# A new front for an attention-and-feed-forward kernel: q and k in long packets, weights cast by the DMA, batch 1 loaded late

## The chip, the cores, the metric

The kernel runs on one core of one Trainium2 chip. Times are device microseconds (us) of one execution, the median of several; one profiled execution gives the trace. The kernel before took 403.1 us (two runs, 402.74 and 403.46). Its runs in the later sets of experiments lay between 400 and 408 us, so kernels are compared by ratios of runs made in the same rounds on the same chip.

## The reference, cut

```python
B, H, S, D = 8, 8, 576, 64
# attention, for each batch and head
out_d     = softmax(scale * mean4(q) @ mean4(k).T) @ mean4(v)         # tokens in fours, then repeated 4 times
out_local = softmax(where(|i - j| < 4, scale * q @ k.T, -1e9)) @ v    # a band of 7 tokens
x = (repeat4(out_d) + out_local) as 4608 tokens x 512                 # heads side by side
# feed forward
h = x @ w_in                      # 512 -> 2048
g = elu(h)
y = g @ w_out                     # 2048 -> 512
```

The feed-forward works on 9 blocks of 512 tokens; the attention makes 576 tokens per batch. So block 0 needs batch 0, block 1 needs batches 0 and 1, block 2 needs batches 1 and 2.

## The kernel before

The work of one pair of heads has fixed steps: load q, k, v (SyncE's queue), cast to fp16 (GpSimd), turn q and k on TensorE and copy them out (ScalarE, VectorE), scores on TensorE, exponentials on ScalarE, a mask on VectorE. Four pairs make a batch: then the denominators (TensorE), their reciprocal (VectorE), its spread over the partitions by a trip through memory, the outputs (TensorE, VectorE), and the sum `xt` on GpSimd, which is the input of the feed-forward. The order in which each engine is given its instructions is written down by hand as a list of times:

```python
def load(b, j):                                # seven DMAs per pair, packets of 256 bytes
    nc.sync.dma_start(out=q32[:], in_=rows(q, 0, NB, 0, QB))
    for src, dst in ((k, k32), (v, v32)):
        nc.sync.dma_start(out=dst[0:96], in_=rows(src, 0, NB, 0, QB))
        ...                                    # 3 tokens of halo on either side, two more DMAs each

def load_weights(i):                           # 16 pieces of 512 KB
    w32 = sb.tile([128, 1024], FP32, tag="w32", bufs=3, name="w32")
    ...
    nc.sync.dma_start(out=w3, in_=src)
    return lambda: nc.gpsimd.tensor_copy(out=to, in_=w3)

def mm1(t, fc):
    tag = "misc" if t < 2 and fc % 2 else "hp"     # four banks in blocks 0 and 1, two later
    hp = ps.tile([128, TBLK], FP32, tag=tag, bufs=2, name="hp")
    ...                                        # 4 matmuls, exp on ScalarE -> e, two VectorE steps -> gt
def mm2(t, i):
    ...                                        # 4 matmuls; every fourth: ScalarE copies op -> os
    nc.sync.dma_start(out=out[r : r + 128, :], in_=os_[:])

at(-100, first)                                # loads of pairs 0 to 2
for n in range(4): ...                         # casts of batch 0
for i in range(8): at(-95, wload, i); at(-95, wcast, i)
for j in range(3): at(-90, load, 1, j); at(-90, wload, 8 + j)
...
for b in range(B):
    base = start_of(b) - 26.5                  # b >= 1: the pairs of batch b run beside the blocks before
    slots, d0, o0 = SLOTS, 16.1, (22.5, 24.1)
    ...
```

The softmax here doesn't subtract the row's maximum and nothing guards it: scores larger than these inputs give would overflow.

## Time and profile before

| stretch of the kernel before | us | length |
|---|---|---|
| attention of batch 0, until the first matmul of block 0's `mm1` | 0 - 44.9 | 44.9 |
| `mm1` of block 0, with pairs of batch 1 | 44.9 - 71.7 | 26.8 |
| `mm2` of block 0, the rest of batch 1, half of batch 2 | 71.7 - 108.1 | 36.4 |
| block 1, until batch 2's denominators are done | 108.1 - 119.0 | 10.9 |
| block 1, until block 2's first matmul | 119.0 - 142.0 | 23.0 |
| blocks 2 to 8 | 142.0 - 401.8 | 259.8 |

The stretches are cut at instructions read from the trace. The first view is from the page of the kernel before: the span in 40 slices of 10.0 us, busy tenths of TensorE, its granted clock, the busy tenths of the DMA engines and the rate in GB/s.

```profile
PE   1465688687986899999999999999899899999996
...
PEclk9999999968999799999999999999999999999999
DMA  6998999965966980796199639926820310100112
GB/s 121 189 253 258 190 215 234 265 126 134 198 139 130 189 176 16 172 231 125 28 195 217 118 78 194 226 64 121 172 79 33 102 53 28 49 29 28 52 54 78
```

TensorE is full from the fifteenth slice on and has holes before; the DMA engines are busy through the whole front. The next view is the same cut into the six stretches: start and end, length, then busy us (and instructions) of TensorE, its weight loads, VectorE, ScalarE, GpSimd, then the granted clock, the mean share of busy DMA engines (the times of all packets are summed, so it can pass 1) and the rate in GB/s.

```profile
0.00:44.90 44.90, 20.86 (x249) 15.71 (x250) 11.92 (x21) 15.36 (x29) 20.64 (x28) 1.00 0.92 203
44.90:71.70 26.80, 22.32 (x152) 10.89 (x151) 22.13 (x37) 14.73 (x28) 16.14 (x21) 1.00 1.12 222
71.70:108.10 36.40, 29.23 (x301) 15.87 (x301) 16.84 (x28) 15.02 (x30) 17.78 (x23) 0.86 0.83 176
108.10:119.00 10.90, 9.84 (x130) 5.98 (x129) 8.28 (x18) 9.61 (x20) 6.92 (x9) 1.00 0.89 169
119.00:142.00 23.00, 17.53 (x176) 9.57 (x173) 17.57 (x33) 11.36 (x22) 8.22 (x12) 0.85 0.81 152
142.00:397.80 255.80, 253.22 (x2055) 127.60 (x2053) 177.69 (x327) 137.14 (x251) 69.03 (x94) 1.00 0.47 105
```

From 142 us on TensorE works 253 of 256 us: only the first 142 us can give much. The chain of waits in the front shows what they are spent on (start, length, what; cut to its longest pieces).

```profile
13.33 4.52 DMA q_105<-in_q_dram
...
23.91 4.83 DMA w_152<-in_moe_w_in_dram
...
28.80 1.07 POOL WI L119
29.89 5.04 DMA w_161<-in_moe_w_in_dram
...
36.05 6.50 DMA w_170<-in_moe_w_in_dram
...
42.61 1.00 POOL WI L119
...
43.69 2.34 POOL xt L352 x3
```

The first feed-forward input `xt` (line 352) is made at 43.69 us, right behind GpSimd's last weight cast (line 119), which waited for the last weight load.

### The profile page before, as it was taken

The numbers are of one execution on the slowest core, as the hardware profiler recorded it, in microseconds if no ns is written. First come the engines' busy times: TensorE is split into PE (matmuls) and PEld (weight loads), VectorE is DVE, ScalarE is ACT, GpSimd is POOL, SyncE is SP. The second block draws the span as 40 slices with busy tenths as digits, with TensorE's granted clock in tenths as the row PEclk, the third lists the DMA queues.
The fourth block names the chain that finished last, engine by engine and source line by source line (L and its number), as shares of the span: only waits on it lengthen the run. The fifth ranks groups of instructions, "written<-read, shape, count | busy, mean of one in ns | idle before, by whom it ended". The sixth has DMA issues, their size and how long they took to land.

```text
span 401.8 us, 8092 instructions
## 1 busy us (share of the span) xinstructions
PE 353.0 (88%) x3052; PEld 185.6 (46%) x3052; DVE 254.4 (63%) x460; ACT 203.8 (51%) x377; POOL 138.7 (35%) x184
## 2 busy tenths in 40 slices
PE   1465688687986899999999999999899899999996
PEld 1352345343553455555545554555454444444442
DVE  0134599732586797697778769886886585555510
ACT  1462157535385376747564855667375334444321
POOL 3365755460850581075028304820450050000000
PEclk9999999968999799999999999999999999999999
DMA  6998999965966980796199639926820310100112
GB/s 121 189 253 258 190 215 234 265 126 134 198 139 130 189 176 16 172 231 125 28 195 217 118 78 194 226 64 121 172 79 33 102 53 28 49 29 28 52 54 78
DMA packets 138082, 53.81 MB, mean 134 GB/s; under 512 B 122580, under 2 KB 131388, under 8 KB 138044
## 3 DMA queue, kind: packets, MB, share of 16 engines
q1 hardware_dynamic: 129420, 47.62, 55.0%
q10 hardware_dynamic: 8624, 5.68, 6.6%
q8 instruction: 24, 0.39, 0.4%
q14 instruction: 14, 0.11, 0.1%
HBM read 43.33 MB, written 9.95 MB: 133 GB/s over the span
## 4 chain that ended last, share of the span: by engine, by line
PE 67%; DMA 12%; POOL 6%; issue 4%; DVE 4%; SPq 3%; ACTq 2%; ACT 1%; POOLq 0%; DVEq 0%
PE op L388 29%; PE hp L368 25%; PE sc L204 2%; PE tk L186 2%; PE tq L176 2%; DVE e L374 2%; PE tq L171 2%; PE lg L325 2%; POOL xt L352 2%; DMA w_170<-in_moe_w_in_dram 2%; DMA rcb<-rd 2%; SPq L149 2%; ACTq L276 2%; DMA w_161<-in_moe_w_in_dram 1%; DMA w_207<-in_moe_w_out_dram 1%
## 5 line engine op out<-in xcount | busy, mean ns | idle before, releaser
L368 PE MATMUL hp<-xt,WI 128*128 128x512 f16 x576 | 150.9, 389 | 4.5 <-DVE gt L377 2.5
L388 PE MATMUL op<-WO,gt 128*128 128x512 f16 x576 | 147.7, 385 | 4.7 <-POOL WO L119 3.8
L373 ACT ACTIVATE e<-hp 128x512 f16<-128x512 f32 x144 | 85.7, 601 | 109.5 <-PE hp L368 90.8
L377 DVE SCALAR_TENSOR_TENSOR gt<-hp,e 128x512 f16<-128x512 f32 x144 | 99.6, 692 | 5.4
L374 DVE TENSOR_SCALAR e<-e 128x512 f16<-128x512 f16 x144 | 63.8, 443 | 51.5 <-ACT e L373 50.5
L368 PEld LDWEIGHTS <-WI 128*128 128x128 f16 x576 | 54.5, 99 | 71.7 <-issue 13.4
L388 PEld LDWEIGHTS <-gt 128*128 128x128 f16 x576 | 54.6, 99 | 68.8 <-issue 7.6
L232 DVE TENSOR_TENSOR mex<-pex,MASK 102x1152 f16<-102x1152 f16 x32 | 29.6, 926 | 40.3 <-ACT pex L222 40.2
L352 POOL TENSOR_TENSOR xt<-ln,gn 128x512 f16<-128x512 f16 (+7 forms) x64 | 42.0, 688 | 34.7 <-DVE ln L343 34.7
L222 ACT ACTIVATE pex<-sc 102x576 f16<-102x576 f32 x64 | 41.4, 647 | 22.3 <-PE sc L214 22.3
L182 ACT CAST qt<-tq 128x720 f16<-128x720 f32 x32 | 24.3, 760 | 30.7 <-PE tq L176 27.3
L394 ACT COPY os<-op 128x512 f32<-128x512 f32 x36 | 21.2, 588 | 25.3 <-PE op L388 25.3
L204 PE MATMUL sc<-qt,kt 64*102 64x96 f16 x384 | 19.1, 226 | 11.5 <-DVE vd L184 6.0
L184 DVE CAST vd<-tq 72x256 f16<-72x256 f32 x32 | 13.2, 413 | 22.3 <-ACT qt L182 22.3
L204 PEld LDWEIGHTS <-kt 64*102 64x102 f16 x384 | 14.4, 135 | 25.8 <-ACT kt L192 12.6
L226 ACT ACTIVATE dex<-sc 72x288 f16<-72x288 f32 x64 | 25.8, 404 | 0.0
L343 DVE TENSOR_TENSOR ln<-lg,rcb 128x576 f16<-128x576 f32 x32 | 23.9, 748 | 0.0
L192 ACT CAST kt<-tk 128x612 f16<-128x612 f32 x32 | 21.8, 680 | 0.1
L176 PEld LDWEIGHTS <-VR 102*72 102x72 f16 x192 | 14.2, 123 | 5.7 <-issue 3.9
L263 DVE RECIPROCAL rc<-den 128x288 f16<-128x288 f32 x8 | 15.6, 1949 | 1.7 <-PE den L257 1.7
L340 DVE TENSOR_TENSOR gn<-lg,rcb 128x144 f16<-128x144 f32 x32 | 9.6, 301 | 5.7 <-POOL xt L352 3.0
L194 DVE CAST kd<-tk 128x144 f16<-128x144 f32 x32 | 9.6, 300 | 1.7 <-ACT kt L192 0.5
(361 smaller groups left out, 265.7 us busy)
## 6 DMA issues: line engine op xcount, KB each, us to landing
out_dram<-os SPq DMA_DIRECT2D x36, 256.0 KB
rcb<-rd ACTq DMA_DIRECT2D x14, 288.0 KB
rcb<-rd ACTq DMA_DIRECT2D x14, 72.0 KB
w_149<-in_moe_w_in_dram SPq DMA_DIRECT2D x1, 512.0 KB
w_152<-in_moe_w_in_dram SPq DMA_DIRECT2D x1, 512.0 KB
w_155<-in_moe_w_in_dram SPq DMA_DIRECT2D x1, 512.0 KB
w_158<-in_moe_w_in_dram SPq DMA_DIRECT2D x1, 512.0 KB
w_161<-in_moe_w_in_dram SPq DMA_DIRECT2D x1, 512.0 KB
```

The lines of the kernel that those rows point to most:

```text
L182: nc.scalar.copy(out=qt[:], in_=tq[:, :, 0 : 3 * QW])
L204: nc.tensor.matmul(sc[e][0:KW, c // 3, QB * (c % 3) : QB * (c % 3) + QB], kt[r, c // 3, c % 3, :], qt[r, c // 3, QW * (c % 3) : QW * (c % ...
L222: nc.scalar.activation(out=pex[:, e, :].rearrange("p (g u) -> p g u", g=2), in_=sc[e][0:KW, :, 0:HB], func=AF.Exp, scale=SCALE,)
L226: nc.scalar.activation(out=dex[:, e], in_=sc[e][0:KG, :, HB : HB + SD], func=AF.Exp, scale=SCALE,)
L232: nc.vector.tensor_tensor(out=mex[:], in0=pex[:], in1=mk2, op=AB.mult)
L343: nc.vector.tensor_tensor(out=ln[:].rearrange("p (g u) -> p g u", g=2), in0=lg[:, :, 0:HB], in1=rcb[:, j, 0:S].rearrange("p (g u) -> p g u ...
L352: nc.gpsimd.tensor_tensor(out=xt(t)[:, j, t0 - TBLK * t : t1 - TBLK * t], in0=ln[:, a:z], in1=_rep4(gn[:, a // 4 : z // 4]), op=AB.add,)
L368: nc.tensor.matmul(hp[:], WI[:, dc, 128 * fc : 128 * fc + 128], x[:, dc, :], start=(dc == 0), stop=(dc == DMC - 1),)
L373: nc.scalar.activation(out=e[:], in_=hp[:], func=AF.Exp)
L374: nc.vector.tensor_scalar(out=e[:], in0=e[:], scalar1=1.0, scalar2=-1.0, op0=AB.min, op1=AB.add)
L377: nc.vector.scalar_tensor_tensor(out=gts[t][:, fc, :], in0=hp[:], scalar=0.0, op0=AB.max, in1=e[:], op1=AB.add)
L388: nc.tensor.matmul(op_[:], gts[t][:, fc, 128 * tt : 128 * tt + 128], WO[:, fc, :], start=(fc == 0), stop=(fc == FCN - 1),)
```

## The change

The intent is to shorten that front. It has three parts.

1. q and k of batches 0 and 1 are loaded as 9 consecutive tokens per partition: packets of 2.3 KB instead of 256 bytes. They are turned in eighteen matmuls of 64 columns each, instead of 6 of 120.
2. The weights are loaded by GpSimd's own queue in 8 pieces of 1 MB, cast to fp16 by the DMA on the way: no loads on SyncE, no casts by GpSimd.
3. Batch 1 is loaded only from the middle of `mm1` of block 0 on: its first tile takes one element of `gt` group 7, so its transfer has to wait for that group.

The order of the work is new with it: batch 0 runs alone; batch 1 runs beside `mm2` of block 0; batch 2 starts only when block 1 starts. Denominators now come as 20 rows of 72 columns per pair, and the reciprocals of batch 1 too are spread by matmuls. The `mm1` of block 1 has two banks instead of four. Two smaller changes come with it: in every batch a pair is loaded by three DMAs instead of seven (k without halo, v with its halo in one transfer), and the constants are loaded by ScalarE's queue.

```diff
+    def nines(b):
+        return b < 2
+    def load_qk(b, j, behind=None):
+            if behind is not None and n == "q":
+                nc.gpsimd.tensor_copy(out=t[0:1, 0:1], in_=behind)
+            if nines(b):
+                t = t[:, 0 : LR * D]
+                ap = [[LR * D, 2 * LP], [1, LR * D]]          # 9 tokens x 64 = 2.3 KB in one piece
+            else:
+                t = t[0:QB, 0:768]
+                ap = [[D, QB], [QB * D, 2 * NB], [1, D]]      # 256 bytes
 ...
-        nc.sync.dma_start(out=w3, in_=src)
-        return lambda: nc.gpsimd.tensor_copy(out=to, in_=w3)
+        nc.gpsimd.dma_start(out=to, in_=src)                  # fp32 -> fp16 on the way
 ...
-        tag = "misc" if t < 2 and fc % 2 else "hp"
+        hp = bank("misc" if t == 0 and fc % 2 else "hp", "hp")
 ...
+    later0 = first_batch()                                    # batch 0 alone; weights behind its q, k, v
+    def second_loads():
+        load_qk(1, 0, gts[0][0:1, 7, 0:1])                    # held until group 7 of mm1
+    for s in range(16):
+        at(T1 + s, mm1, 0, s)
+    at(T1 + 7.6, second_loads)
+    T2 = T1 + 17
+    for j in range(NPAIR):
+        at(T2 + 4 * j, early_turn, 1, j, nc.scalar.copy)
+        at(T2 + 4 * j + 2, scores, 1, j)
 ...
+        if b == 2:
+            base, slots, d0, o0 = 0, (0, 1.5, 3, 4.5, 6, 7.5, 9, 10.5), 11.2, (17, 18)
+            for j in range(3):
+                at(-20 + j, load_qk, b, j)                    # behind mm2's last output writes on SyncE
+                at(-20 + j, load_v, b, j)
+        elif b == 3:
+            base, slots, d0, o0 = 12, (0, 1.6, 3, 4.6, 6.2, 8, 10, 11.6), 12.3, (19, 20.5)
         else:
-            base = start_of(b) - 26.5
+            base = start_of(b) - 26
```

## The prediction

> **What bounds the kernel now.** By the stage table, the stages up to 142 us (attention of batch 0; first matmul of block 0; its second; first of block 1) hold 99.8 us of TensorE work, so 42 us are idle. From 142 to 398 us TensorE is 99% busy. Only the front can give much. The first 45 us are a DMA front: DMA share 0.92, nearly all packets under 512 B (256 B took 18 ns by the median, 1 KB 46), seven issues on SyncE per head pair. The chain of waits runs there through k/q loads, SyncE issues, weight loads and GpSimd's weight casts (16 of 1.04 us); the last input-weight cast ends at 43.65 us, and only then GpSimd makes the first xt. At 72-108 us GpSimd waits for weight and q/k/v loads.
>
> **What changes, costed.**
> - q, k of batches 0, 1: 2.3 KB packets. From 2 KB packets (86-98 ns) I estimate 0.8 us per tensor instead of 1.5; no halo issues. Batch 0's score loop is then paced by ScalarE, about 4 us per pair (exponentials 2.1, copy 0.7, waits), ending near 22 us instead of 33.
> - Weights leave SyncE's queue and GpSimd's casts. The Trainium skill, "DMA: Bandwidth & Descriptors", section "SWDGE vs HWDGE vs iDMA", says a cast in a DMA needs GpSimd's queue; no run here shows its speed yet. Estimate from 2 KB packets: 3 us per MB, input weights in by about 33 us.
> - Denominators: 96 matmuls of 72 columns instead of 36. At the 22 ns per small matmul seen warm: 2.1 us instead of 1.1 per batch (2.5 us more while cold). Reciprocal: 1.95 us to an estimated 0.5.
> - Batch 1 is loaded from the middle of block 0; its pairs run serially against 12 pieces of the second matmul, about 5.3 us per pair.
> - Batch 2's loads stand behind block 0's output writes on SyncE, its transposes before block 1 on TensorE. I expect a hole of about 8 us.
>
> **Critical path, sum.** All first xt ready: 37 us (now 48.6). Block 0 first matmul, VectorE-paced at 0.93-1.1 us per group: 18 us, to 55 (now 72). Batch 1 with the second matmul: 22 us of pairs, 7 to the reciprocal, 12 of outputs and the hole: to 96 (now 108). Block 1 with batch 2 and half of batch 3: 33 us, to 129 (now 142). The rest is TensorE-bound: 260 us now, less 3.6 of work moved ahead, plus about 4 of denominators: 260. Sum **389 us**, range **377 to 400**. The front gains near 20 us early and gives back almost half around batches 1 and 2.
>
> **Chances:** faster by over 2% 0.72, within 2% 0.24, slower 0.04.
>
> **What would show it.** Batch 0's scores done near 22 us; no weight casts on GpSimd; first mm1 group at 35-39 us, its sixteenth at 55; TensorE idle 5-9 us before block 1, released by batch 2's q or v load; denominators near 2.1 us; block 2 starting near 129; then 258-262 us to the end; about 18,000 DMA packets fewer.
>
> **What would make it wrong.** The casting DMA much slower than 3 us per MB, or its issue holding GpSimd several us each (then batch 0's last v cast, the adds and batch 1's loads slip: 395-400). VectorE's 16-bit operations and GpSimd blocking each other (here a 0.28 us operation once took 2.40 us beside GpSimd's adds). Batch 2's loads ready earlier, or small matmuls overlapping better: 377-382. ScalarE freed from two of four spread transfers per batch might also shorten the steady blocks, whose 37.8 us exceed their TensorE work of about 36.7.

## The result, and the profile after

The changed kernel took **396.97 us** (two runs, 396.93 and 397.0), against 403.1. The ratio is **0.985** (95% interval 0.982 to 0.988). A ratio is the mean time of one kernel's fast runs over that of the other's of the same rounds, so it isn't quite the ratio of the medians quoted. The kernel is 1.5% faster: within the predicted range of times, against a predicted gain of 3.5%.

The same cuts side by side, with the lengths that the prediction named:

| stretch | before | predicted | after | after minus predicted |
|---|---|---|---|---|
| all of the first `xt` ready | 48.6 | 37 | 34.1 | -2.9 |
| from there to the end of block 0's `mm1` | 23.1 | 18 | 15.4 | -2.6 |
| from there to block 1's first matmul | 36.4 | 41 | 42.5 | +1.5 |
| **block 1, to block 2's first matmul** | 33.9 | **33** | **46.7** | **+13.7** |
| rest | 259.8 | 260 | 256.4 | -3.6 |
| span of the profile | 401.8 | 389 | 395.1 | +6.1 |

The lead over the kernel before is 22 us when `mm1` of block 0 ends, 16 us when block 1 starts, and 3 us when block 2 starts. Of these 19 us, 6 go before block 1 (the prediction had planned for a loss there), and most go in one place: block 1 takes 12.8 us longer than before. The page of the changed kernel, in slices of 9.9 us:

```profile
PE   2778988948876898899999999999999999999996
...
PEclk9999999686997899999999999999999999999999
DMA  8989993069999997977784958543000500100112
GB/s 262 170 131 144 238 276 105 2 126 200 200 183 154 163 201 136 190 151 153 138 192 94 181 127 177 115 96 103 29 28 30 128 28 28 53 27 36 46 53 80
```

In the first slice the transfers run at 262 GB/s, 79% of the bytes in the 2.3 KB packets, where they ran at 121 in the first and 189 in the second slice before, mostly in packets of 256 bytes. But in the eighth slice they stand at 2 GB/s (a busy share of 0 tenths), where the kernel before moved 265. The stretches of the changed kernel, with the columns as before:

```profile
0.00:31.60 31.60, 20.09 (x433) 16.52 (x434) 16.33 (x27) 13.97 (x29) 14.38 (x29) 1.00 0.88 189
31.60:49.50 17.90, 16.98 (x64) 6.75 (x64) 13.56 (x31) 8.96 (x15) 6.36 (x11) 1.00 1.03 191
49.50:92.00 42.50, 31.53 (x516) 19.05 (x516) 17.58 (x30) 18.53 (x42) 17.16 (x24) 0.85 0.63 132
92.00:116.20 24.20, 19.82 (x261) 10.51 (x260) 17.83 (x34) 17.49 (x35) 12.32 (x15) 0.91 1.22 193
116.20:138.70 22.50, 17.28 (x199) 10.19 (x200) 12.92 (x27) 10.12 (x19) 7.83 (x12) 0.85 1.00 164
138.70:391.40 252.70, 249.59 (x2328) 126.73 (x2326) 166.56 (x321) 134.53 (x249) 69.06 (x92) 1.00 0.48 101
```

Compare the fourth and fifth lines with those of before: from batch 2's denominators to block 2 takes 22.5 us after 23.0, but from block 1's start to the denominators takes 24.2 us after 10.9. **All of the 13 us are lost before batch 2's denominators.** TensorE is busy 19.8 of those 24.2 us, twice its time before: there is more to do, and some of it at half clock (0.91 granted).

Groups of the changed kernel that answer to terms of the prediction (line, engine, operation, shapes, count; busy us, mean ns; idle time before):

```profile
L374 PE MATMUL den<-mex,IND 112*32 112x72 f16 x512 | 8.1, 212 | 3.0 <-DVE mex L348 3.0
...
L380 DVE RECIPROCAL rc<-den 128x72 f16<-128x72 f32 x8 | 4.8, 602 | 3.4 <-PE den L374 3.4
...
L146 POOL DMA_DIRECT2D WI<-in_moe_w_in_dram x4 | 3.1, 798 | 0.0
...
L146 POOL DMA_DIRECT2D WO<-in_moe_w_out_dram x4 | 3.0, 774 | 0.0
```

The casting transfers hold GpSimd 3 us per set of four and land 8.6 us (input weights) and 9.2 us (output weights) after their issue by the median, so this part did what it should: the packets of the four input-weight transfers run from 22.8 to 35.1 us with next to nothing beside them, 3.1 us per MB of fp32 (3 predicted). In the kernel before the reciprocal took 1949 ns. And the chain of waits through block 1, cut to the pieces that matter:

```profile
82.01 0.59 ACT os L524
82.62 0.33 SPq L526
...
83.52 0.68 SPq L165
...
84.28 5.55 DMA v<-in_v_dram
...
89.89 0.83 POOL v L211
...
100.20 1.04 PE hp L498 x4
101.26 0.61 ACT e L503
...
102.43 0.40 ACT dex L339
102.82 0.55 ACT pex L333
103.39 0.76 DVE mex L348
104.18 0.82 DVE e L504
105.02 0.70 DVE gt L507
...
117.26 4.80 DMA rd<-rc
122.08 6.82 DMA rcb<-rd
```

It reads: ScalarE copies block 0's last outputs (`os`) at 82.01 us, SyncE can then write them, and only behind those writes come batch 2's loads (line 165); the first pair's v lands at 89.83. Then follow rounds of 5.0 to 5.6 us, one per pair, in which the `mm1` groups wait for `gt` on VectorE, `gt` stands behind the mask `mex`, and `mex` waits for ScalarE's exponentials. Last comes the trip of the reciprocals through memory. The view of SyncE's own waits, from 50 to 92 us, shows the first of these once more (total, times, longest):

```profile
SPq L526 <- ACT os L524: 22.2, 3, 15.7
```

Finally the pairs, by the start of their scores (read from the trace):

| | before | after |
|---|---|---|
| pairs scored before block 1's first matmul | 10 | 8 |
| pairs of batch 2 still to score then | 2 | 4 |
| eighth, ninth, tenth pair | 83.0, 90.5, 97.1 | 67.6, 95.5, 101.2 |
| casts of q, batch 2 | 82.0, 84.3, 87.0, 108.2 | 87.0, 91.6, 96.3, 100.9 |

The changed kernel scores its eighth pair 15 us earlier than the kernel before and its ninth 5 us later: for 28 us no pair is scored.

### The profile page after: what moved, and what is told of

Read it like the earlier page. It is cut to its first block, busy times and chain, and to the rows that moved or that the text cites. A ratio compares the mean times of both kernels' runs of the same rounds, so it can differ in the third digit from the quotient of the medians.

```text
span 395.1 us, 9269 instructions
## 1 busy us (share of the span) xinstructions
PE 355.3 (90%) x3792; PEld 189.8 (48%) x3792; DVE 244.8 (62%) x468; ACT 204.2 (52%) x389; POOL 127.1 (32%) x181
## 3 DMA queue, kind: packets, MB, share of 16 engines
q1 hardware_dynamic: 107082, 39.33, 49.5%
## 4 chain that ended last, share of the span: by engine, by line
PE 70%; DMA 14%; ACT 5%; DVE 5%; POOL 2%; issue 2%; ACTq 1%; SPq 0%; POOLq 0%; DVEq 0%
PE op L518 30%; PE hp L498 26%; DMA v<-in_v_dram 4%; DMA rd<-rc 4%; PE lg L438 2%; PE sc L311 2%; ACT pex L333 2%; DMA rcb<-rd 2%; PE tq L285 2%; DVE gt L507 2%; PE den L374 2%; DMA SEL<-SELc 2%; PE tq L223 2%; PE tk L223 1%; DMA q<-in_q_dram 1%
## 5 line engine op out<-in xcount | busy, mean ns | idle before, releaser
L465 POOL TENSOR_TENSOR xt<-ln,gn 128x64 f16<-128x64 f16 (+7 forms) x64 | 42.1, 688 | 122.2 <-DVE ln L458 122.2
L333 ACT ACTIVATE pex<-sc 112x576 f16<-112x576 f32 x64 | 41.0, 647 | 14.5 <-PE sc L321 10.3
L348 DVE TENSOR_TENSOR mex<-pex,MASK 112x1152 f16<-112x1152 f16 x32 | 27.0, 843 | 25.6 <-ACT pex L333 25.3
L259 ACT CAST qt<-tq 128x720 f16<-128x720 f32 x24 | 18.3, 763 | 29.9 <-PE tq L285 27.6
L211 POOL CAST v<-v 112x768 f16<-112x768 f32 x32 | 28.7, 898 | 12.1 <-DMA v<-in_v_dram 12.1
L204 POOL CAST q<-q 96x768 f16<-96x768 f32 x24 | 20.8, 868 | 33.2 <-issue 21.2
L524 ACT COPY os<-op 128x512 f32<-128x512 f32 x36 | 21.2, 588 | 17.9 <-PE op L518 17.5
L311 PEld LDWEIGHTS <-kt 64*112 64x112 f16 x384 | 14.5, 140 | 18.1 <-issue 5.5
L311 PE MATMUL sc<-qt,kt 64*112 64x96 f16 x384 | 18.9, 231 | 4.5 <-ACT dex L339 1.4
L204 POOL CAST k<-k 96x768 f16<-96x768 f32 x24 | 20.3, 847 | 4.4 <-DMA k<-in_k_dram 4.4
L223 PE MATMUL tq<-I,q 96*128 96x120 f16 x144 | 12.1, 222 | 8.8 <-POOL q L204 5.0
L285 PEld LDWEIGHTS <-VR 112*72 112x72 f16 x192 | 15.2, 132 | 5.7 <-issue 3.9
```

Source lines behind the costliest of these rows:

```text
L204: nc.gpsimd.tensor_copy(out=t, in_=x.rearrange("p (e c d) -> p c e d", e=2, d=D))
L211: nc.gpsimd.tensor_copy(out=t[:], in_=st32.pop(("v", b, j)).rearrange("p (e c) d -> p c e d", e=2))
L311: nc.tensor.matmul(sc[e][0:KW, c // 3, QB * (c % 3) : QB * (c % 3) + QB], kt[r, QB * c : QB * c + KW], q_of(b, j, r, c), start=True, stop= ...
L333: nc.scalar.activation(out=stS[(b, j)][2][:, e, :].rearrange("p (g u) -> p g u", g=2), in_=sc[e][0:KW, :, 0:HB], func=AF.Exp, scale=SCALE,)
L348: nc.vector.tensor_tensor(out=mex[:], in0=pex[:], in1=mk2, op=AB.mult)
L465: nc.gpsimd.tensor_tensor(out=xt(t)[:, j, t0 - TBLK * t : t1 - TBLK * t], in0=ln[:, a:z], in1=_rep4(gn[:, a // 4 : z // 4]), op=AB.add,)
```

## The experiments

Eighteen more runs were made. The quoted texts were written before their runs; the letters of theories are those of that moment. In the end these remained: **P**, block 1 is set by the number of pairs that the engines take through it; **L**, by batch 2's own chain; **C**, by TensorE's half clock after it stood idle; **D**, by the arrival of batch 2's data. Three lengths are read from each profile: from block 1's `xt` ready to the end of batch 2's denominators ("to den"), from there to block 2's first matmul ("den to block 2"), and the start of block 2.

| kernel | median us | ratio to before [95%] | to den | den to block 2 | block 2 starts |
|---|---|---|---|---|---|
| before | 403.1 | 1 | 10.8 | 23.0 | 142.0 |
| changed | 396.97 | 0.985 [0.982, 0.988] | 29.1 | 22.5 | 138.7 |
| changed, again | 395.49 | 0.980 [0.973, 0.987] | 29.0 | 25.1 | 138.5 |
| nines_off | 407.11 | 1.009 [1.001, 1.018] | 29.9 | 22.9 | 147.0 |
| w_sync | 404.68 | 1.003 [0.994, 1.012] | 29.1 | 22.6 | 142.0 |
| b1_free | 398.96 | 0.983 [0.978, 0.989] | (slow) | (slow) | (slow) |
| b2_early | 392.04 | 0.970 [0.964, 0.975] | 29.3 | 19.5 | 133.3 |
| b2_pe | 397.84 | 0.972 [0.963, 0.981] | 29.1 | 22.6 | 137.1 |
| b2_early_pe | 395.46 | 0.977 [0.969, 0.985] | 29.4 | 23.0 | 136.5 |
| b2_nines | 394.14 | 0.974 [0.969, 0.979] | 29.6 | 22.4 | 136.5 |
| hp4 | 394.91 | 0.977 [0.969, 0.986] | 28.2 | 21.4 | 133.0 |
| hp4_early | 390.87 | 0.967 [0.959, 0.975] | 29.1 | 21.2 | 136.2 |
| b3_late | 405.56 | 1.005 [0.995, 1.015] | 27.2 | 19.3 | 135.9 |
| b2_overlap | 398.62 | 0.985 [0.975, 0.996] | | | 136.6 |
| b2_overlap_hp4 | 395.7 | 0.978 [0.967, 0.989] | | | (slow) |
| b3_two_gone (wrong result) | 395.54 | 0.980 [0.974, 0.986] | 27.9 | 23.2 | 135.6 |
| b2_two_gone (wrong result) | 395.91 | 0.979 [0.973, 0.985] | 28.5 | 22.9 | 135.2 |
| warm | 395.44 | 0.977 [0.972, 0.982] | 29.5 | 20.9 | 135.7 |
| b2_two_unloaded (wrong result) | 389.29 | 0.960 [0.953, 0.967] | 19.3 | 24.3 | 132.3 |
| warm_hp4_early | 390.03 | 0.965 [0.957, 0.972] | 28.0 | 19.4 | 133.5 |

The kernel before had medians of 404.1 to 405.7 us beside these runs. All but the three marked were correct. Medians are over all runs, ratios over fast ones. Fast executions of one kernel differ by 2 to 6 us, so steps of 1% between two rows aren't told apart.

### The parts of the change, one at a time

**after_again**: the changed kernel once more, beside the second set of runs, no edit.

> The changed kernel as it is, run beside the next three on the same chip, to give them a reference. All theories: 0.985 of the time before, as measured first, within 0.5%.

It measured 0.980. Its intervals and those of the first measurement overlap; 0.980 to 0.985 is the level against which the others are read. Its block 1 took 48.7 us in the profile.

**nines_off**: without part 1.

```diff
     def nines(b):
-        return b < 2
+        return False
 ...
-        copy_nines(qt[:, 0:S], tq, nc.scalar.copy)
-        copy_nines(kt[:, PAD : PAD + S], tk, copy_k)
-        add_fours(b, j)
+        copy_q(b, j, tq, nc.scalar.copy)
+        copy_k_(b, j, tk, copy_k, nc.vector.tensor_copy)
```

> The changed kernel with q and k of batches 0 and 1 loaded as in the other batches (96 partitions, 256 B packets), all else kept. If the packet size makes the front: q and k of batch 0 take 1.5 us each instead of 0.8, the weights come 5-6 us later, the first xt are ready at 37-41 us instead of 31.7, and since block 1 onward is one chain the whole shift stays: total 0.995-1.005 of before. If the gain comes from the rest (no weight casts, no halo issues): first xt at 33-35, total 0.98-0.99.

Measured 1.009: the long packets, with the turning that goes with them, are worth 2.5 to 3%. The first `xt` is ready at 37.2 us (31.7 in the profile of after_again) and block 1 starts at 99.7 (89.8): about 5 us are lost with batch 0 and as much again with batch 1.

**w_sync**: without part 2: fp32 pieces by SyncE, cast by GpSimd.

```diff
-        nc.gpsimd.dma_start(out=to, in_=src)
+            w3 = stage("w32")[:].rearrange("p (c m) -> p c m", c=src.shape[1])
+            nc.sync.dma_start(out=w3, in_=src)
+            wq.append((to, w3))          # nc.gpsimd.tensor_copy later
```

> The changed kernel with the weights loaded as fp32 halves of 512 KB by SyncE behind batch 0 and cast by GpSimd (16 casts of 1.04 us), as before, all else kept. If the casting DMA matters for the front: GpSimd casts wait for the loads ahead of the first adds, first xt at 40-44 us, total 1.00-1.01 of before. If it only moves work off an idle engine: first xt within 3 us of 31.7, total 0.98-0.985.

Measured 1.003: the casting transfers are worth about 2%. Here too the first `xt` slips, to 36.8 us. Either part alone leaves the new order about as slow as the old one; it pays only with both.

**b1_free**: without part 3.

```diff
-        load_qk(1, 0, gts[0][0:1, 7, 0:1])
+        load_qk(1, 0)
 ...
-    at(T1 + 7.6, second_loads)
+    at(T1 - 0.5, second_loads)
```

> Changed kernel without the third part of the change: batch 1's loads are issued before block 0 and aren't held until its 8th group of hidden units. If holding them matters (their packets would delay the weights of mm2 and the first outputs), block 0 and mm2 of block 0 start later by over 1 us; if not, the start of mm1 of block 0 is within 1 us of 29 to 31.6 and the ratio is the changed kernel's, .98 to .985. My estimate: no difference over 2 us either way; batch 1's first pair is turned up to 2 us earlier, since its loads no longer end just before.

Measured 0.983, the level of the changed kernel: holding batch 1 back neither helps nor hurts by an amount that these runs resolve. The profile fell in the slow state, so its stages aren't compared, and the guess of 2 us for batch 1's first pair stays untested.

### Batch 2's chain: loads, spread, banks

**b2_early**: batch 2's first three pairs are put into SyncE's queue before block 0's last output writes.

```diff
-                at(-20 + j, load_qk, b, j)
-                at(-20 + j, load_v, b, j)
+                at(T2 + 9 + 0.1 * j, load_qk, b, j)
+                at(T2 + 9 + 0.1 * j, load_v, b, j)
```

> The changed kernel, with the loads of batch 2's first three pairs issued before the last output writes of block 0 on SyncE. Theory L (block 1 grew from 33.9 to 46.7 us because batch 2's loads start only at 83 us and then feed one pair per 4.7 us): block 1 starts at 86-88 us, denominators of batch 2 are done near 105-107 us instead of 116, block 2 starts at or before 130 (now 138.7), total 386-389. Theory S (the DRAM round trip of the reciprocals, 117.3 to 132.3 us beside the loads of batch 3, sets block 2's start): only the hole before block 1 goes, the trip stays 13 us or more, block 2 starts at 134 or later, total 391-394. Theory E (ScalarE and VectorE pace the pairs at about 5 us each whatever the loads do): pairs stay 5 us apart, gain is the 4-5 us of the hole alone, total about 392.

Measured 0.970, the largest gain of a single edit, though not told apart from b2_pe's 0.972 or b2_nines's 0.974. Two lines show what was filled: the stretch from 62 to 83 us, first of the changed kernel, then of b2_early (columns as above; the last two are DMA share and GB/s).

```profile
62.00:83.00 21.00, 18.31 (x323) 11.18 (x321) 9.56 (x17) 9.19 (x24) 3.06 (x5) 0.84 0.08 28
```

```profile
62.00:83.00 21.00, 15.15 (x300) 9.56 (x300) 9.06 (x17) 9.34 (x24) 3.77 (x4) 0.92 0.99 169
```

But the gain came at another place than the loads' own: "to den" stayed at 29.3 us, though the first three pairs' data were there (their casts followed each other at 0.8 us). The pairs then took 6 us each on the engines. The 3 us came from "den to block 2", 19.5 after 22.5: the first VectorE step of the outputs followed the denominators after 13.2 us instead of 16.1, with the DMA share in that stretch at 0.78 instead of 1.00.

The trace also shows where the earlier data was lost again. Counted from the ready `xt`, the first pair's scores began after 6.3 us instead of 8.5, but the three rounds that followed took 18.4 us instead of 16.3. With the data there, GpSimd casts a pair's q, k and v one right behind the other, and the VectorE step on `e` (line 504) beside these casts takes 1.59 us, twice in this chain of waits:

```profile
99.54 1.59 DVE e L504
...
105.87 1.59 DVE e L504
```

In the changed kernel, where the casts stand apart, the longest such step in this stretch took 0.82 us. All seven profiles of kernels with early loads have at least one of 1.58 us or more there, and in all others the longest is 0.97 us. This is read from the traces: no run moved the casts.

**b2_pe**: batch 2's reciprocals are spread by matmuls instead of the trip through memory.

```diff
-        at(base + d0 + 0.5, spread_out, b)
-        at(base + d0 + 1.5, spread_in, b)
+        if b == 2:
+            at(base + d0 + 0.5, spread_pe, b, 0)
+            at(base + d0 + 1.5, spread_pe, b, 2)
```

> The changed kernel, with batch 2's reciprocals spread by matmuls and ScalarE copies (as for batches 0 and 1) instead of a write to DRAM and two reads. Theory S: the 15 us from reciprocal to first product become 4-6, ScalarE is not blocked for 3.8 us by the wait for the write, block 2 starts at 129-132 us, total 387-390. Theory L: the pairs of batch 3, late like those of batch 2, hold TensorE instead; gain 3 us at most, total 394-396. Theory E: 3.7 us of added ScalarE copies eat most of it, total 393-396.

The ratio of its two fast runs is 0.972, with two slow runs beside them; the profile shows nothing gained in block 1: "den to block 2" 22.6, and the outputs begin 16.3 us after the denominators without any trip. The trip alone is not the limit: the outputs also stand behind five groups of `mm1`, a piece of `mm2` and two pairs of batch 3 in TensorE's order.

**b2_early_pe**: both edits together.

> Both edits together. If L and S are separate costs in one chain, the gains add: block 2 starts at 124-127 us and the total is 381-385. If one hides behind the other, the total is that of the better one alone, 386-389. If E holds, not below 389.

Measured 0.977, no better than either one. Gains of single repairs do not add up here.

**b2_nines**: batch 2 too in packets of 2.3 KB (`b < 3`, with the matching copies).

> The changed kernel, with batch 2's q and k also loaded as 9 tokens per partition (2.3 KB packets), which shortens a pair's loads but costs VectorE 1.5 us of sums and TensorE 24 more matmuls per pair. Theory L: pairs arrive every 3.2 us instead of 4.7, block 1 starts 1-2 us earlier, batch 2's denominators near 109 us, total 390-393. Theory S: a smaller gain, through less traffic beside the trip, 393-396. Theory E: VectorE is loaded more, total unchanged or up to 3 us slower, 396-400.

Measured 0.974, with "to den" at 29.6: shorter transfers alone don't shorten it either.

**hp4**: four banks for block 1's hidden units again, as in the kernel before.

```diff
-        hp = bank("misc" if t == 0 and fc % 2 else "hp", "hp")
+        hp = bank("misc" if t < 2 and fc % 2 else "hp", "hp")
```

> The changed kernel with one condition set back: block 1's first matmul again alternates between the misc and the hp banks (4 instead of 2), as in the kernel before. Theory H (with two hp banks TensorE waits for VectorE's gt before each group, and the score matmuls stand behind that group, so the pair cycle of 5.5 us includes VectorE's queue): the waits of hp on gt in block 1 go, pairs come every 4.5-5 us, block 1 takes 41-44 us instead of 46.7, total 3-5 us less than the changed kernel. Theory P (block 1 is long because it now holds 6.5 head pairs instead of the 4 of before, at 5.5 us each through the two double banks and ScalarE): pairs stay near 5.5 us apart, total within 1.5 us of the changed kernel.

Measured 0.977. The pairs come 4.9 us apart instead of 5.4, as the chain shown above suggests, and block 2 starts at 133.0. The casts of q come 5.1 us apart, waiting for their data, and each pair's scores begin 8.6 to 8.9 us after its cast of q; in the changed kernel that lag grows from 8.5 to 10.8 us. So, by these traces, the transfers set the pace with four banks, and the engines with two. Block 1 took 43.9 us, as theory H had it; the time, 1 us less than the changed kernel's in the same set, isn't what H had, and the interval overlaps that of the changed kernel.

**hp4_early**: hp4 and b2_early.

> Four banks, and batch 2's loads issued before the last output writes. Theory H: in the early-load run the pairs were 6.3 us apart with 1.5 us of each in waits of hp on gt; without them 4.8-5.2, block 1 starts near 88 and block 2 near 126-129 us, total 386-388 at the first chip's scale (0.958-0.963 of before). Theory P alone: about 0.97 of before, as the early loads alone gave.

Measured 0.967, about b2_early's 0.970. In the profiled execution (a span of 392.5 us, the longest of the four) block 2 started at 136.2; its three rounds took 5.6 to 5.9 us, each with a step on `e` of 1.58 us beside GpSimd's casts.

### Moving pairs to another place

**b3_late**: early loads; batch 3's pairs moved behind block 1, batches 2 and 3 spread by matmuls, outputs earlier.

```diff
-  (b == 2)  ..., 11.2, (17, 18)
+  (b == 2)  ..., 11.2, (14, 15)
-            base, slots, d0, o0 = 12, (0, 1.6, 3, 4.6, 6.2, 8, 10, 11.6), 12.3, (19, 20.5)
+            base, slots, d0, o0 = 19, (0, 1.5, 3, 4.5, 6, 7.5, 9, 10.5), 11.2, (14, 15.5)
```

> Early loads for batch 2; batch 3's head pairs moved out of block 1 into block 2; batches 2 and 3 spread by matmuls so that no DRAM trip stands in the way; batch 2's outputs three slots earlier. Theory P: block 1 then holds 4 pairs and takes 45.3 less 2.5 times 5.5, so 31-34 us, block 2 starts at 119-122 us; block 2, where TensorE has twice the dense work per pair, grows from 37 to 41-44 us; total 382-387 (0.95-0.96 of before). Theory H: block 1 still waits on gt, 36-39 us. If something else (the outputs' chain, GpSimd's adds) sets block 2's start, block 1 stays above 40 us and the total above 390.

Measured 1.005, a miss. Block 1 still took 43 us, with four pairs in it instead of seven, and block 2 took 50 us with the pairs it was given. A half-clock stretch of 27.3 us from 68 us on lay in the profiled run, so this run alone couldn't settle the size of P.

**b2_overlap**: early loads; batch 2's first two pairs placed in batch 1's tail, all of batch 3 in block 1.

> Theory G: the front's lead is lost because the stream of head pairs stops. In the changed kernel the last pair of batch 1 is scored at 67.6 us and the first of batch 2 at 95.5, 28 us in which no pair advances (7.5 us in the kernel before), while pairs on either side come every 5-6 us in both kernels. This run loads batch 2 early and places its first two pairs between the denominators and outputs of batch 1, and everything after two pairs' slots sooner. G: the gap shrinks to about 12 us, block 1 starts 2-5 us later than 90 but with two pairs done, block 2 starts 8-11 us earlier than in the changed kernel on this chip (127-130), total 0.955-0.965 of before (385-390). If instead the work only moves (TensorE, ScalarE and VectorE as the limit of the whole front), block 2 starts within 3 us of 138 and the total is that of the early loads alone, about 0.97.

Measured 0.985: its first two pairs were scored at 75.6 and 85.2 us, block 2's `xt` was ready at 124.8, and block 2 nevertheless began only at 136.6, because batch 3's pairs now filled block 1. The work had only moved.

**b2_overlap_hp4**: the same with four banks.

> The same with four hp/misc banks in block 1. G and H together: one to four us below b2_overlap, 0.950-0.960 of before. If H is nothing, equal to b2_overlap.

Measured 0.978; the profile isn't read.

### Taking work away on purpose

Since moving work only moved the limit, the next kernels leave work out. Their outputs are wrong, which doesn't matter for the times.

**b3_two_gone** and **b2_two_gone**: the turning and scoring of the first two pairs of batch 3, or of batch 2, are left out; loads and casts stay. Their outputs are made from two other pairs' probabilities.

```diff
+            if b == 3 and j < 2:                 # b2_two_gone: b == 2
+                at(base + slots[2 * j + 1], as_of, b, j)
+                continue
             at(base + slots[2 * j], transposes, b, j)
             at(base + slots[2 * j + 1], scores, b, j)
```

> Changed kernel with the turning and scoring of batch 3's first two pairs left out of block 1 (their outputs are then made from batch 2's last two pairs, so the result is wrong on purpose; loads, casts, denominators, outputs and weights are kept). Block 1 took 46.7 to 48.7 us in the two profiles of the changed kernel. Theory P (block 1 is long because 6.5 pairs go through it at about 5 us each): block 1 falls by two pairs, to 36 to 39 us, and the kernel by 8 to 11 us against the changed one (ratio to before about .955). Rival L (block 1 is long because of batch 2's own chain: four pairs in a row from the late loads on, denominators, a 15-us trip through memory, outputs; batch 3's pairs only fill waits): block 1 stays at 43 us or more and the kernel gains under 4 us (ratio .97 or more).

> The same with batch 2's first two pairs left out instead (their outputs are made from batch 1's last two pairs, wrong on purpose), which is where the kernel before stood when its block 1 began: two pairs of batch 2 done. Theory P: the same as with batch 3's pairs out, block 1 36 to 39 us. Rival L: here block 1 does fall, by two pairs of 5.5 us, to 35 to 37 us, since the denominators come 11 us earlier, while with batch 3's pairs out it doesn't. If neither falls, a third cause holds block 1.

P had block 1 shorter by two pairs in both runs, L only without batch 2's pairs. Without batch 3's two pairs block 1 still took 45.5 us, against P. Its chain of waits shows why: from the denominators on it is the trip through memory that holds it.

```profile
113.43 4.35 DMA rd<-rc
...
118.51 8.74 DMA rcb<-rd
```

Without batch 2's two pairs the denominators should have come 11 us earlier, but "to den" went only from 29 to 28.5, against P and L. Block 1's first matmul came at 80.3 us in that run, 10 us sooner than in b3_two_gone and warm beside it, and block 2 at 135.2 after their 135.6 and 135.7: filling the hole in front of block 1 gained nothing there. GpSimd's casts of q came at 83.7, 88.5, 93.2, 98.0, 102.7 and 107.5 us: one pair in 4.75 us, in a steady beat, nearly every cast waiting for its data. The line for the stretch from the ready `xt` to the denominators is

```profile
83.80:112.30 28.50, 18.21 (x203) 9.47 (x202) 14.88 (x28) 11.79 (x22) 15.08 (x18) 0.74 1.35 197
```

with a DMA share of 1.35 at 197 GB/s, while TensorE is busy 18 of 28.5 us. A pair's q, k and v are 288, 288 and 336 KB in the list of transfers; 934,000 bytes at 197 GB/s take 4.7 us, which is the beat.

**b2_two_unloaded**: as b2_two_gone, and those two pairs are not loaded or cast either.

```diff
-            for j in range(3):
+            for j in (2, 3):
                 at(-20 + j, load_qk, b, j)
 ...
+            if b > 2 or j > 1:
                 at(when, cast_qk, b, j)
                 at(when, cast_v, b, j)
```

> As the run that left out the turning and scoring of batch 2's first two pairs, but now without their loads and casts either (wrong on purpose, outputs from batch 1's last two pairs). In that run GpSimd's casts came 4.75 us apart per pair from 83.7 us on, each waiting for its data, with the transfers at about 200 GB/s: one pair's q, k, v are 912 KB, so 4.7 us. Theory D (block 1's front is paced by the arrival of q, k, v, because the transfers stood idle from 63 to 83 us): the denominators of batch 2 end 8 to 10 us earlier than 112.3, at 102 to 105, and block 2 starts at 125 to 129 instead of 135.2. Rival L' (order of the instructions, the trip through memory, half clock): the denominators end at 109 or later and block 2 starts within 3 us of 135.

Measured 0.960 after 0.979 without the two loads left out. In absolute times the forecast missed (denominators at 108.0, block 2 at 132.3), because the front of this profiled run was already 4.9 us later (`xt` ready at 88.7 instead of 83.8). Counted from there, "to den" fell from 28.5 to 19.3 us, by 9.2, which is two pairs of the beat, and block 2 came 7.8 us sooner. The stretch, with the transfers as full as before:

```profile
88.70:108.00 19.30, 13.81 (x201) 7.84 (x201) 15.15 (x28) 11.58 (x22) 9.92 (x13) 0.94 1.36 195
```

So D holds for the kernel with the pairs' engine work taken away. It isn't the only limit of the changed kernel: b2_early has the data in time and still needs 29.3 us.

Together: data late and four pairs of work 29.0 to 29.1; data early and four pairs of work 29.3; data late and two pairs of work 28.5; two pairs less of both 19.3. No run had early data and two pairs of work. **Two limits of nearly equal size lie side by side, the transfers at 4.7 us per pair and the round through the engines at 5 to 6 us; taking either away alone gained about 1 us of this stretch at most.** The size of the second is read from the traces, and it isn't fixed: early data itself lengthens the round.

### The clock, and the best version

**warm**: 42 matmuls of 512 columns that nobody reads, where TensorE stands idle around block 1.

```diff
+        if (b, j) == (2, 0):
+            warm(tq[:, 0, :], 20)        # nc.tensor.matmul(to, WI[:, 0, 0:128], WI[:, 1, 0:512]) 20 times
 ...
+            if b == 2:
+                warm(d[:], 10)
 ...
+        if b == 3:
+            at(base + slots[2] - 0.05, lambda: warm(bank("misc", "wm")[:], 12))
```

> Changed kernel with 42 matmuls of 512 columns whose results nobody reads, put where TensorE stands idle: 20 before batch 2's first turning, 10 before its denominators, 12 before the turning of batch 3's second pair. Theory C (idle stretches of TensorE bring half clock, and half clock stretches the stage after): the half-clock windows at 86 (10.2 us) and 124 (6.8 us) go or shrink, block 1 shortens by 3 to 5 us, ratio .970 to .975. If the clock is only a companion: the windows shrink but block 1 stays within 1.5 us of 46.7 to 48.7, ratio .98 to .985.

The half-clock stretch at 86 us shrank from 10.2 to 6.8 us and the one at 124 us went. "Den to block 2" took 20.9 us and block 1 44.9, 2 to 4 us less than in the two profiles of the changed kernel. The ratio, 0.977, is on the lower side of 0.980 to 0.985, but the intervals overlap: in the time of the kernel the effect of the clock isn't told from nothing.

**warm_hp4_early**: fillers, four banks and early loads together.

> The three repairs together: batch 2's first three pairs loaded while the transfers stood idle, four banks for block 1's hidden units as in the kernel before, and the idle stretches of TensorE filled with matmuls nobody reads. Early loads alone measured .9695, four banks alone .9773, both .9671, fillers alone .9768. If their causes are separate: block 2 starts at 130 to 133, 388 to 390 us, ratio about .962. If the front is limited by several things of nearly equal size, which theory D with engines at 5 us per pair says: no better than .965 to .97. Either way faster than both kernels.

Measured 0.965 [0.957, 0.972], 390.03 us, block 2 at 133.5. It has the lowest ratio of the correct kernels, not told apart from hp4_early and b2_early. It beats both the kernel before and the changed kernel, by 3.5% and 1.5 to 2%. That the three don't add up is what two parallel limits would do.

## Why the prediction was right or wrong

**What was right.** The bound was right: a front of transfers and casts, with 260 us of full TensorE behind it. Batch 0's last scores began at 20.8 us (predicted to be done near 22); the first `xt` was ready at 34.1 (37); `mm1` of block 0 ended at 49.5 (55); TensorE stood idle for 5.0 and 2.1 us just before block 1, waiting for batch 2's casts of q and v (5 to 9 us predicted, released by a load of q or v); no weight is cast on GpSimd; the casting transfers took 3.1 us per MB (3); 21,800 packets fewer (18,000). Both main parts of the change are worth 2 to 3% each when taken away.

**What was wrong: the step "Block 1 with batch 2 and half of batch 3: 33 us, to 129 (now 142)".** It took 46.7 us. This one term is 13.7 us too small; the others together were 7.6 us too large, so the span missed by 6.1. That the time still lay inside the range is owed to these errors of opposite sign, which is luck; the outcome itself, within 2%, had been given 0.24. The prediction shows no working for the 33 us; they lie within 1 us of the length of block 1 before, 33.9 us. But the kernel before began its block 1 with two of batch 2's pairs already scored and the q and k of a third cast. The changed kernel begins with none scored and batch 2's loads issued 9 us before. The window before held 2 pairs up to batch 2's denominators, the window after 4: 10.9 us against 24.2, and the whole lost time lies there. The expression "the front gains near 20 us early and gives back almost half" had the right shape; it gives back nearly all.

**Why those pairs were missing there.** From 67.6 to 95.5 us no pair is scored. Batch 1's pairs run serially in front of this gap, and batch 2's loads, which the prediction did place behind the output writes on SyncE, wait there until 83 us while the transfers stand nearly idle (a share of 0.08 from 62 to 83 us). The prediction costed this as a hole of about 8 us before block 1. The hole was that size; what it didn't cost was the time after it, in which four pairs arrive at 4.7 us each and pass the engines at 5.4.

**What the runs showed of the cause.** Shown: where the time was lost (all before batch 2's denominators); that the arrival of data sets the pace once the engines' work is taken away (28.5 to 19.3 us); that early data alone doesn't shorten that stretch (29.3), and that the kernel with it is 1 to 1.5% faster, 3 us of it in the next stretch of the profile. P alone, L alone and the trip alone fell, each in its own run. Argued only: that the round of 5.0 to 5.6 us through `gt`, `mex` and the exponentials is the second limit. The chain of waits shows it, and four banks brought the pairs from 5.4 to 4.9 us apart, where the data's beat (5.1 us) took over; but no run took the round away with the data early. Read from the traces only: that early data lengthens the round to about 6 us, by steps on `e` that wait beside GpSimd's casts. The prediction had named this blocking among its risks.

**Smaller points.** The denominators were costed as 2.1 us instead of 1.1; they took 0.95 us for the warm ones, less than before (1.16). The estimate took 22 ns per small matmul; these go to four column groups in turn, and about 10 ns each came out (0.95 us for 93). The reciprocal took 0.60 us (estimated 0.5). The rest took 256.4 us where 260 had been forecast. The operation of 2.40 us that the prediction puts beside GpSimd's adds stood beside three casts (at 49.88 us); the longest beside adds took 2.30 us.

**What stays open.** How much of block 1 is due to the half clock: by the records 17 us around block 1 ran at half clock in the first profile of the changed kernel and 24 us in the second, and filling the holes changed the profile by 2 to 4 us, but not the time beyond the noise. What early loads are worth once GpSimd's casts are kept apart from the steps on `e`. And the clock at the very start: the records give full clock for the first stretch, though batch 0's denominators took 1.63 us there and 0.97 us from batch 4 on.

## What to carry to other kernels

When a change moves work out of one stage, cost the next stages by the work they will hold, counted in units (here pairs of heads), not by the length that their window had before. A lead in the front is kept only if the loads of the next stage use the time won: look for slices in which the transfers stand idle, and for loads that stand in a queue behind writes which wait for something else. Where single repairs each gain little, leave out two suspected costs at once, with a wrong result if need be: two limits side by side show only together.

## What the Trainium skill lacked or had wrong

- "DMA: Bandwidth & Descriptors", section "SWDGE vs HWDGE vs iDMA", says that a cast during a DMA needs GpSimd's queue, and gives no time for one. Here four casting transfers of 1 MB fp32 held GpSimd for 3.1 us in all, 0.8 us per issue, and landed 8.6 to 9.2 us after their issue by the median. The section "Anatomy of one DMA" has 2.0 us plus the bytes over 436 GB/s, an estimate of 4.4 us for 1 MB alone; the four for the input weights shared the engines with each other only and took 3.1 us per MB together.
- "TensorE: Matmul & The Clock Gate", section "Part 1: The HAM clock gate", has an idle window of about 3.4 us. The runs agree: half-clock stretches of 3.4, 6.8 and 10.2 us. It speaks of full clock after one busy window, though it warns that the clock has been seen stuck. In b3_late 27.3 us of half clock came in one piece, although TensorE was busy for 21.4 of 27.5 us there, 16.6 us of them without a gap above 60 ns (68.5 to 85.1 us).
- The same page, "Back-to-back issue gap", gives an issue floor of about 25 ns for up to 64 columns, and "Part 3: Packing small matmuls — row/col tiling" about 4 ns between starts in different tiles. Here the denominators' matmuls of 72 columns, in turn on four column groups, started 2 to 5 ns after the one before in two of three cases and up to about 25 ns after it in most others, so the trace agrees with the second. Neither section states what costing such a long series needs, the mean: about 10 ns per matmul.
- "SBUF — State Buffer", section "Who interferes with whom", says that in VectorE's two-port modes it and GpSimd block each other, and that the second to issue waits for the whole of the other's instruction. The traces show more than one instruction of waiting: the step on `e` took 0.28 us alone, 2.40 us beside three of GpSimd's casts in a row in the kernel before (49.88 us), 2.30 us beside four adds (287.31 us), and 1.58 us beside casts in b2_early. The page doesn't say that instructions one behind the other on GpSimd can hold VectorE through all of them.
